# Pooled attention with a SiLU MLP behind it: dummy matmuls tied to a key slot, a fourth PSUM bank for one early group, and two weight loads put ahead of a query load

## The chip, the cores and the metric

The kernel runs on one core of a Trainium2 chip. The metric is the device time of one execution in microseconds (us); smaller is better. The runs of the kernel before took 285.24, 285.42, 285.84 and 285.95 us, median 285.63. One more execution was taken with the hardware profiler, and the views below are of that one.

## The reference

Attention over pooled keys and values, then a two-layer MLP on its output:

```python
k_p = k.reshape(B, H, Sp, pool, D).mean(axis=3)      # B, H = 8, 8; S = 576; D = 64; pool = 8; Sp = 72
v_p = v.reshape(B, H, Sp, pool, D).mean(axis=3)
scores = scale * np.matmul(q, k_p.transpose(0, 1, 3, 2))
...
attn = softmax(scores)
x = np.matmul(attn, v_p)                             # to 4608 x 512
h = x @ w_in                                         # 512 x 2048
g = h * (1.0 / (1.0 + np.exp(-h)))
out = g @ w_out                                      # 2048 x 512
```

The inputs are float32. The kernel works in bfloat16 with float32 accumulation.

## The kernel before, in words

**Tiling.** The 4608 tokens are worked on in nine tiles of 512 (`t` = 0 to 8). For each tile, `up` computes the first product in 16 groups of 128 hidden columns (`plain`, line 541: four matmuls of 128 x 128 weights into one PSUM tile `hp_ps`, then one SiLU activation on ACT, line 547, to `h_T`). Then `down` (tile 0) or `down_quarters` (the others, with seven block products in place of eight) computes the second product. The attention of batch `t + 1` is spread between those matmuls as *fillers*: `spread` runs each filler once the given number of matmul steps has gone by. The order on each engine is the order of the program text; nothing is rescheduled.

**Prologue.** The attention of batch 0 cannot hide behind anything and is computed first, in halves. The raw keys of a batch are 4608 rows (head, pooled row) of 512 values, loaded as five *slots* of 128 rows, the last one with 64. Slots 0 and 1 of the keys come in one transfer on the SP queue, slots 2 and 3 in two transfers on the ACT queue, and slot 4 on SP (lines 700 to 703). `slot_sums` (lines 263 to 272) adds the eight rows of each pooled key on DVE: `slot_sums("k", 0)` takes slots 0 to 2, in place over the first half of each row, then over the first quarter. `select_k` (line 290) places the sums by head on PE, `copy_k` takes them out of PSUM, `q_transpose` (line 153, DVE) turns the queries, `scores` (line 345, PE, then four exponentials on ACT, line 353), `denominators` (line 363, PE; then logarithm and exponential on ACT, or a reciprocal on DVE, line 369), and `numerators` (line 389, PE, then a multiplication on DVE into `xT`, line 398).

**Dummy matmuls.** `warm_up(n)` issues n matmuls of zeros, 128 x 128 weights with 512 columns in bfloat16, into `warm_ps`, which nobody reads. Nineteen stand ahead of `select_k(0, 0)`, and small numbers between the later steps of the prologue.

**PSUM banks.** The eight banks are split in two sets: three for the tag "mm" (`hp_ps`, `warm_ps`, a few of the prologue's tiles) and five for "at" (scores, denominators, numerators, placed keys). Which bank a tile gets is settled when the program is built: the pool gives it the bank that it reckons to be free first. So it isn't a strict rotation. In the program of before, the last four score tiles of the prologue lie in the "at" banks 5, 4, 7 and 3, where a strict order of use would have put 3 before 7. The two denominators that `up` computes for the second halves lie in banks 6 and 5, the numerators behind them in 4 and 7, and in 3 and 6, and the next placed keys in bank 5. The instructions of all engines stand in the program in the order in which the pool's planning took them up; there the second reciprocal (line 369) ends behind the SiLU of the fourth group.

**Tile 0 of `up`.** Its items are groups 0 to 10 on the first 288 tokens, then groups 0 to 10 on the other 224, then groups 11 to 15 on all 512. Its fillers: denominators behind the 2nd and the 6th matmul, numerators behind the 14th and the 18th, placed keys of batch 1 behind the 73rd and the 81st, query transposes behind the 83rd to the 89th. `moe_tables` (line 408) loads the activation table with SiLU just ahead of it.

**The POOL queue.** All other loads are issued by POOL in the order of the text. At the end of the prologue this is: keys of batch 1 in three transfers (lines 767 to 769), `load_q(1)` (576 KB written), `load_w_in(1536, d_ff)` (two transfers of 256 KB; the first-product weights of groups 12 to 15), three quarters of the second-product weights, values of batch 1, the last quarter of the second-product weights.

Of the kernel before, what the change touches and what calls it, by code (L numbers as in the profile page):

```python
# [27 lines left out]
FP32 = mybir.dt.float32  # L28
# [8 lines left out]
def kernel(  # L37
# [9 lines left out]
    nc = tc.nc  # L47
# [6 lines left out]
    d_ff = moe_w_in.shape[1]  # L54
# [27 lines left out]
    singles = ctx.enter_context(tc.tile_pool(name="singles", bufs=1))  # L82
# [8 lines left out]
    def ps_tile(shape, dtype, tag, name):  # L91
        return psum.tile(shape, dtype, tag=tag, bufs=banks[tag], name=name)
# [4 lines left out]
    ident = shifts[:, SP : SP + 128]  # L97
    ones = singles.tile([SP, 32], BF16, name="ones")
    warm = singles.tile([128, 512], BF16, name="warm")
    w_in_sb = singles.tile([128, KF, d_ff], BF16, name="w_in_sb")  # L100
    w_out_sb = singles.tile([128, KG, d_model], BF16, name="w_out_sb")
    w_sum = singles.tile([128, 5, KQ, CQ], BF16, name="w_sum")
# [26 lines left out]
    def load_q(b, halves=False):  # L129
        st = batches.setdefault(b, {})  # L130
        q_bf = mid.tile([128, 2, QI * D], BF16, tag="q_bf", name="q_bf")
        if halves:
            pass
        elif b == B - 1:

            for s in range(4):
                for a in range(2):
                    nc.gpsimd.dma_start(
                        out=q_bf[QP * s : QP * (s + 1), a, :].rearrange(
                            "p (i d) -> p i d", d=D  # L140
                        ),
                        in_=q[b, 4 * a + s].rearrange("(i p) d -> p i d", p=QP),
                    )
        else:
            nc.gpsimd.dma_start(out=q_bf, in_=q_r[b])
        st["q_bf"] = q_bf
        st["qT"] = mid.tile([128, 2, QI, 2, QP], BF16, tag="qT", bufs=1, name="qT")
# [13 lines left out]
    def raw_tile(tag, heads, full=False):  # L161
        raw = big.tile([128, H * PH], FP32, tag=tag, name="raw")
        if full:
            return raw
        return raw[:SP, : H * PH].rearrange("k (h e) -> k h e", h=heads)
# [45 lines left out]
    def k_transpose(b, parts=(0, 1)):  # L211
        st = batches[b]
        kT_ps = ps_tile([128, 2, 2, SP], FP32, "at", "kT_ps")
        for a in parts:
            for c in range(2):
# [10 lines left out]
    RE = POOL * D  # L226
# [7 lines left out]
    SA = SLOTS - 1  # L234
    row_tiles = {
        n: [
            big.tile([128, m, RE], FP32, tag=f"{n}_raw2", name="raw") if i else
            raw_tile(f"{n}_raw", H, full=True)[:, : m * RE].rearrange(
                "r (i e) -> r i e", e=RE
            ) for i, m in enumerate((SA, SLOTS + 1 - SA))  # L240
        ] for n in "kv"
    }


    def load_slots(eng, b, name, i0, i1, half=None):
        es = slice(0, RE) if half is None else slice(half * RE // 2, (half + 1) * RE // 2)
        src = (k if name == "k" else v)[b].rearrange("h (sp p) d -> (h sp) (p d)", p=POOL)
        src = src[:, es]
        how = dict(accum_op=ALU.add) if half else {}
        tiles = row_tiles[name]  # L250
        w = es.stop - es.start
        if i0 == SLOTS:
            eng.dma_start(
                out=tiles[1][:REST, SLOTS - SA, :w], in_=src[128 * SLOTS :], **how
            )
        else:
            j = i0 // SA
            eng.dma_start(
                out=tiles[j][:, i0 - SA * j : i1 - SA * j, :w],
                in_=src[128 * i0 : 128 * i1].rearrange("(i r) e -> r i e", r=128), **how  # L260
            )

    def slot_sums(name, j, halves=False):
        raw = row_tiles[name][j]
        dst = rows5[name][:, SA:] if j else rows5[name][:, :SA]
        w = RE // 4 if halves else RE // 2
        while w > D:
            nc.vector.tensor_add(  # L268
                out=raw[..., :w], in0=raw[..., :w], in1=raw[..., w : 2 * w]
            )  # L270
            w //= 2
        nc.vector.tensor_add(out=dst, in0=raw[..., :D], in1=raw[..., D : 2 * D])
# [131 lines left out]
    def attn_tables():  # L404
        nc.scalar.preload_act_table_set("natural_log_exp_and_others")
# [59 lines left out]
    def up(t, fillers, items):  # L465
# [57 lines left out]
        for it in items:  # L523
            if len(it) == 3:
                plain(t, step, *it)
            else:
                for n in it[1]:
                    stage(it[0], n)
# [1 line left out]
            pass  # L530

    def plain(t, step, g, n0, n):
        hp_ps = ps_tile([128, 512], FP32, "mm", "hp_ps")
        c0 = (t * NTT + n0) % NX

        for r0, r1 in ((0, min(n, NX - c0)), (min(n, NX - c0), n)):
            for kk in range(KF) if r1 > r0 else ():
                if r0 == 0:
                    next(step)
                x0 = (c0 + r0) % NX  # L540
                nc.tensor.matmul(  # L541
                    hp_ps[:, r0:r1],
                    lhsT=w_in_sb[:, kk, g * 128 : (g + 1) * 128],
                    rhs=xT[:, kk, x0 : x0 + r1 - r0],
                    start=(kk == 0), stop=(kk == KF - 1),
                )
        nc.scalar.activation(h_T[:, g, n0 : n0 + n], hp_ps[:, :n], func=AF.Silu)  # L547
# [146 lines left out]
    warm_ps = ps_tile([128, 512], FP32, "mm", "warm_ps")  # L694

    def warm_up(n):
        for _ in range(n):
            nc.tensor.matmul(warm_ps, lhsT=warm[:, :128], rhs=warm, start=True, stop=True)

    load_slots(nc.sync, 0, "k", 0, 2)  # L700
    load_slots(nc.scalar, 0, "k", 2, 3)
    load_slots(nc.scalar, 0, "k", 3, 4)
# [6 lines left out]
    load_slots(nc.gpsimd, 0, "v", 4, 5)  # L709
    attn_tables()  # L710
    nc.vector.memset(warm, 0.0)
    nc.vector.memset(ones, float(POOL))
    nc.vector.memset(kp, 0.0)
    nc.gpsimd.memset(shifts, 0.0)
# [5 lines left out]
    def load_w_in(c0, c1):  # L720
        for g in range(2):
            nc.gpsimd.dma_start(
                out=w_in_sb[:, 2 * g : 2 * g + 2, c0:c1], in_=w_in_r[g][:, :, c0:c1]
            )
# [6 lines left out]
        load_w_in(512 * c, 512 * (c + 1))  # L731

    act_copy = nc.scalar.copy
    warm_up(19)
    slot_sums("k", 0)
    select_k(0, 0)
    copy_k(0, 0, act_copy)
# [29 lines left out]
    load_slots(nc.gpsimd, 1, "k", 0, 3)  # L767
    load_slots(nc.gpsimd, 1, "k", 3, 4)
    load_slots(nc.gpsimd, 1, "k", 4, 5)
    load_q(1)  # L770
    load_w_in(1536, d_ff)
    for c in range(3):
        load_w_out(c)
    load_slots(nc.gpsimd, 1, "v", 0, 3)
# [142 lines left out]
```

The softmax here doesn't subtract the row's maximum and nothing guards it: scores larger than these inputs give would overflow.

## Time and profile before

| what | value |
|---|---|
| median of four runs | 285.63 us |
| the profiled execution's own time | 285.44 us |
| its span, first to last instruction | 283.5 us |
| around the span | 1.94 us |
| PE busy | 276.6 us (98%) |
| DVE busy | 225.6 us (80%) |
| ACT busy | 183.6 us (65%) |
| DMA share, 5 to 40 us | 1.07 to 1.24 of sixteen engines' time |
| mean granted TensorE clock | 1.000 |

Rows of the order-of-time view start with the time from the span's start and the duration, both in us; then engine, line, operation, output and input tiles, shape, how many instructions were merged, and in brackets how long the engine was idle before, and who ended that. The rows of PEld are weight loads, those of PE the matmuls. Durations of matmuls include the way through the array, so the next one starts before the one before has ended: the distance between starts is the rate.

### The profile page before, as it was taken

To read this page: it belongs to the slowest core of one execution; us is meant where nothing else is said; L and a number is where in the kernel's file an instruction comes from. 1 tells how busy PE (TensorE), PEld (TensorE's weight loads), DVE (VectorE), ACT (ScalarE), POOL (GpSimd) and SP (SyncE) were. 2 spreads that over 40 slices of the span, in tenths; PEclk is the share of its full clock that TensorE was granted. 3 is DMA by queue.
4 is the path that set the end of the run, shared out by engine and by line. 5 is a ranking of instruction groups with operands and counts; after the bars stand their busy time and mean duration, and the time that the engine had idled before them with its cause. 6 is when DMAs were issued, how large, how long until landed. Compare 5 with 4: busy or idle time off the path is not lost.

```text
span 283.5 us, 6909 instructions
## 1 busy us (share of the span) xinstructions
PE 276.6 (98%) x2793; PEld 194.4 (69%) x2793; DVE 225.6 (80%) x404; ACT 183.6 (65%) x359; POOL 60.8 (21%) x78
## 2 busy tenths in 40 slices
PE   8889999999999999999999999999999999999995
PEld 2338544466777677767898786688667766787684
DVE  4987836899978898879896988799888786836773
ACT  1667766568567876687668856885779467326700
POOL 8754316242140214021402130541000000000000
PEclk9999999999999999999999999999999999999999
DMA  7999998896739863995498539696830032005003
GB/s 209 281 265 229 214 314 153 233 168 114 148 53 189 187 140 48 177 204 116 66 180 189 104 84 184 128 147 102 148 87 0 2 97 53 2 18 132 1 19 132
DMA packets 31376, 37.70 MB, mean 133 GB/s; under 512 B 10352, under 2 KB 22256, under 8 KB 31344
## 3 DMA queue, kind: packets, MB, share of 16 engines
q0 software_dynamic: 23840, 26.77, 52.5%
q1 hardware_dynamic: 6928, 9.58, 12.5%
q10 hardware_dynamic: 576, 0.92, 0.9%
q8 instruction: 22, 0.36, 0.6%
q14 instruction: 10, 0.08, 0.1%
HBM read 36.70 MB, written 9.44 MB: 163 GB/s over the span
## 4 chain that ended last, share of the span: by engine, by line
PE 90%; DVE 3%; DMA 3%; POOL 1%; ACT 1%; issue 1%; DVEq 0%; POOLq 0%
PE hp_ps L541 25%; PE o_psP L649 15%; PE o_psQ L649 15%; PE u_psP L482 7%; PE u_psQ L482 7%; PE o_psR L649 5%; PE sc_ps L345 4%; PE o_ps L576 3%; DMA raw<-in_v_dram 3%; PE nu_ps L389 2%; PE u_psR L482 2%; PE den_ps L363 2%; DVE xT L398 1%; DVE w_sum L627 1%; POOL q_bf L127 1%
## 5 line engine op out<-in xcount | busy, mean ns | idle before, releaser
L541 PE MATMUL hp_ps<-xT,w_in_sb 128*128 128x512 bf16 (+3 forms) x412 | 82.6, 340 | 0.5 <-ACT h_T L547 0.4
L649 PEld LDWEIGHTS <-h_sum 128*128 128x128 bf16 x640 | 60.6, 98 | 11.9 <-issue 1.3
L547 ACT ACTIVATE h_T<-hp_ps 128x512 bf16<-128x512 f32 (+2 forms) x95 | 51.4, 546 | 25.3 <-PE hp_ps L541 24.2
L541 PEld LDWEIGHTS <-w_in_sb 128*128 128x128 bf16 x412 | 39.4, 98 | 24.9 <-issue 1.4
L609 DVE TENSOR_TENSOR h_sum<-h_T 128x1024 bf16<-128x1024 bf16 (+1 forms) x72 | 50.8, 743 | 6.9 <-ACT h_T L547 6.9
L353 ACT ACTIVATE es<-sc_ps 72x384 bf16<-72x384 f32 (+1 forms) x100 | 39.0, 469 | 10.2 <-PE sc_ps L345 10.1
L482 PEld LDWEIGHTS <-w_sum 128*128 128x128 bf16 x300 | 29.3, 98 | 7.7
L649 PEld LDWEIGHTS <-h_T 128*128 128x128 bf16 x256 | 24.1, 98 | 4.4 <-issue 0.9
L398 DVE TENSOR_TENSOR xT<-nu_ps,rec 128x384 bf16<-128x384 f32 (+1 forms) x50 | 23.9, 531 | 0.2
L372 ACT ACTIVATE lnd<-den_ps 128x384 f32<-128x384 f32 (+1 forms) x23 | 11.1, 484 | 19.3 <-PE den_ps L363 19.3
L153 DVE STREAM_TRANSPOSE qT<-q_bf 128x576 bf16<-128x576 bf16 x32 | 23.0, 754 | 0.1
L490 ACT ACTIVATE h_T<-c_sb 128x512 bf16<-128x512 f32 x30 | 18.1, 626 | 5.7 <-DVE c_sb L514 5.7
L177 POOL DMA_DIRECT2D raw<-in_k_dram x5 | 7.1, 1430 | 52.9 <-DMA raw<-in_k_dram 52.9
L268 DVE TENSOR_TENSOR raw<-raw 128x384 f32<-128x384 f32 (+3 forms) x20 | 12.3, 617 | 7.7 <-DMA raw<-in_v_dram 4.7
L553 POOL DMA_DIRECT2D out_dram<-o_sb x1 | 0.6, 617 | 79.7 <-issue 79.7
L649 PE MATMUL o_psP<-w_out_sb,h_sum 128*128 128x256 bf16 x128 | 17.6, 273 | 0.0
L514 DVE TENSOR_TENSOR c_sb<-u_psP,t_sb 128x512 f32<-128x512 f32 x15 | 10.3, 688 | 8.2 <-PE u_psP L482 3.6
L649 PE MATMUL o_psQ<-w_sum,h_sum 128*128 128x256 bf16 x128 | 16.7, 273 | 0.0
L649 PE MATMUL o_psQ<-w_out_sb,h_sum 128*128 128x256 bf16 x128 | 16.6, 273 | 0.0
L649 PE MATMUL o_psQ<-w_sum,h_T 128*128 128x256 bf16 x128 | 16.5, 273 | 0.0
L649 PE MATMUL o_psP<-w_sum,h_T 128*128 128x256 bf16 x128 | 16.5, 273 | 0.0
L649 PE MATMUL o_psR<-w_sum,h_sum 128*128 128x256 bf16 x128 | 15.7, 273 | 0.0
(80 smaller groups left out, 439.6 us busy)
## 6 DMA issues: line engine op xcount, KB each, us to landing
out_dram<-o_sb SPq DMA_DIRECT2D x128, 64.0 KB, 4.3
raw<-in_k_dram POOLq DMA_DIRECT2D x10, 576.0 KB, 10.0
raw<-in_v_dram POOLq DMA_DIRECT2D x10, 576.0 KB, 8.5
q_bf<-in_q_dram POOLq DMA_DIRECT2D x6, 576.0 KB, 13.6
w_in_sb<-in_moe_w_in_dram POOLq DMA_DIRECT2D x8, 256.0 KB, 8.4
w_out_sb<-in_moe_w_out_dram POOLq DMA_DIRECT2D x4, 512.0 KB, 13.6
raw<-in_v_dram POOLq DMA_DIRECT2D x2, 768.0 KB, 11.3
raw<-in_k_dram POOLq DMA_DIRECT2D x1, 768.0 KB, 10.3
```

Source lines behind the costliest of these rows:

```text
L153: nc.vector.transpose(out=st["qT"][:, a, f * QF : (f + 1) * QF].rearrange("r i c p -> r (i c p)"), in_=st["q_bf"][:, a, f * n : (f + 1) * n],)
L268: nc.vector.tensor_add(out=raw[..., :w], in0=raw[..., :w], in1=raw[..., w : 2 * w])
L345: nc.tensor.matmul(sc[s][:, cs], lhsT=kz[b % 2][rows, g, c, :], rhs=st["qT"][rows, g, i0:i1, c, :], start=(c == 0), stop=(c == 1),)
L353: nc.scalar.activation(es[:, s, :], sc[s], func=AF.Exp, scale=score_scale)
L372: nc.scalar.activation(lnd, den_ps[:, :w], func=AF.Ln)
L398: nc.vector.tensor_mul(out=xT[:, 2 * g0 + c : 2 * (g0 + ng - 1) + c + 1 : 2, cols], in0=nu[c][:, :w].rearrange("r (g n) -> r g n", g=ng), ...
L482: nc.tensor.matmul(ps[bank][:, u, :], lhsT=w[:, kk, 128 * u : 128 * (u + 1)], rhs=x[:, kk, :], start=first and u == 0 and kk == 0, stop=kk ...
L490: nc.scalar.activation(h_T[:, g : g + 2, j * NQ : (j + 1) * NQ], src, func=AF.Silu)
L541: nc.tensor.matmul(hp_ps[:, r0:r1], lhsT=w_in_sb[:, kk, g * 128 : (g + 1) * 128], rhs=xT[:, kk, x0 : x0 + r1 - r0], start=(kk == 0), stop= ...
L547: nc.scalar.activation(h_T[:, g, n0 : n0 + n], hp_ps[:, :n], func=AF.Silu)
L609: nc.vector.tensor_tensor(out=h_sum[n][:, ks, :], in0=quarter(*a, ks), in1=quarter(*b, ks), op=op)
L649: nc.tensor.matmul(ps[b][:, c, :], lhsT=left(n, kt, c), rhs=W_OUT[n][:, kt, :], start=b not in begun, stop=kt == k1 - 1, skip_group_check= ...
```

## The change

Three edits, all around the prologue.

1. Of the 19 dummy matmuls ahead of `select_k(0, 0)`, nine stay. Behind them come eight of a new kind: float32, weights `warm32` (zeros, 128 x 128), with the last 128 columns of slot 2 of the raw keys as the moving operand, still into `warm_ps`. They read what a transfer writes, and so wait for it. `warm32` is set to zero by one more memset on DVE.
2. The `hp_ps` tile of group 3 of tile 0 on its first 288 tokens takes a bank of "at" in place of one of "mm".
3. `load_w_in(1536, d_ff)` is issued ahead of `load_q(1)`.

```diff
+    warm32 = singles.tile([128, 128], FP32, name="warm32")
...
     def plain(t, step, g, n0, n):
-        hp_ps = ps_tile([128, 512], FP32, "mm", "hp_ps")
+        tag = "at" if (t, g, n0) == (0, 3, 0) else "mm"
+        hp_ps = ps_tile([128, 512], FP32, tag, "hp_ps")
...
+    def warm_behind(rhs, n):
+        for _ in range(n):
+            nc.tensor.matmul(
+                warm_ps[:, : rhs.shape[-1]], lhsT=warm32, rhs=rhs, start=True, stop=True
+            )
+
...
     nc.vector.memset(warm, 0.0)
+    nc.vector.memset(warm32, 0.0)
     nc.vector.memset(ones, float(POOL))
...
-    warm_up(19)
+    warm_up(9)
+    warm_behind(row_tiles["k"][0][:, SA - 1, RE - 128 :], 8)
     slot_sums("k", 0)
...
     load_slots(nc.gpsimd, 1, "k", 4, 5)
+    load_w_in(1536, d_ff)
     load_q(1)
-    load_w_in(1536, d_ff)
     for c in range(3):
         load_w_out(c)
```

## The prediction

> **What bounds the kernel now.** I read the chain of work that ended last first, then PE's waits, then the order-of-time view of the two places that the change touches, then the transfers.
>
> ```profile
> PE 90%; DVE 3%; DMA 3%; POOL 1%; ACT 1%; issue 1%; DVEq 0%; POOLq 0%
> ```
>
> ```profile
> PE kz_ps L290 <- DVE k L272: 0.5, 1, 0.5
> PE hp_ps L541 <- ACT h_T L547: 0.4, 1, 0.4
> ```
>
> From about 20 us on the chain is PE nearly without a break, and PE's waits over the whole span list nothing later than the one on `h_T`. So one rule carries the sum: what PE saves or loses by 21.6 us reaches the end at full size, unless something behind it comes late. Before that the chain is not PE's: it runs from the landing of the values at 13.05 over DVE (sums, multiplications, a query transpose) to the last scores at 16.41, four exponentials, the table load, and the first SiLU.
>
> The first place:
>
> ```profile
> 1.20 5.71 PE L698 MATMUL warm_ps<-warm 128*128 128x512 bf16 x19 [1.20 <-DVE warm L711]
> ...
> 4.15 2.26 PEld L698 LDWEIGHTS <-warm 128*128 128x128 bf16 x11 [0.27 <-issue]
> ...
> 5.40 1.55 DVE L268 TENSOR_TENSOR raw<-raw 128x768 f32<-128x768 f32 x2 [2.78 <-DMA raw<-in_k_dram]
> ...
> 6.99 0.36 DVE L272 TENSOR_TENSOR k<-raw 128x192 bf16<-128x192 f32 x1
> ...
> 7.40 0.28 PE L290 MATMUL kz_ps<-shifts,k 128*32 128x72 bf16 x12 [0.50 <-DVE k L272]
> ```
>
> The weight loads of the dummies start 0.43 us apart until 4.15, then eleven start within 2.26 us, 0.215 apart: the array ran at half rate for the first 2.95 us, though the granted-clock row shows 1.00 there, so I go by the spacing. The dummies end at 6.91, and PE waits 0.50 for DVE's key sums. Those began at 5.40, when slots 0 and 1 had landed (issued 0.74, 4.6 us). Nothing that PE does before 7.40 moves 7.40 forward.
>
> The second place:
>
> ```profile
> 17.93 3.77 DVE L369 RECIPROCAL rec<-den_ps 128x288 f32<-128x288 f32 x2 [0.86 <-PE den_ps L363]
> ...
> 18.20 1.28 ACT L408 ACT_TABLE_LOAD   x1
> ...
> 18.64 0.91 PE L541 MATMUL hp_ps<-xT,w_in_sb 128*128 128x288 bf16 x6
> ...
> 19.49 1.01 ACT L547 ACTIVATE h_T<-hp_ps 128x288 bf16<-128x288 f32 x3
> ...
> 19.95 0.41 PE L541 MATMUL hp_ps<-xT,w_in_sb 128*128 128x288 bf16 x2 [0.41 <-ACT h_T L547]
> ...
> 21.11 0.41 ACT L547 ACTIVATE h_T<-hp_ps 128x288 bf16<-128x288 f32 x1 [0.60 <-PE hp_ps L541]
> ...
> 21.24 0.43 PE L389 MATMUL nu_ps<-es,vp 72*32 72x288 bf16 x8
> ...
> 21.61 6.14 PE L541 MATMUL hp_ps<-xT,w_in_sb 128*128 128x288 bf16 x55
> ```
>
> PE has filled three "mm" banks by 19.55 and stands still until the first SiLU, held by the table load, gives one back.
>
> **Part 2, the fourth bank.** Group 3's tile comes from "at" and need not wait. The last six matmuls of the row at 18.64 are 0.12 us apart (288 columns at the 0.215 per 512 of above), so the seventh can start at 18.64 + 6 x 0.12 = 19.36 instead of 19.95. From there the order on PE is unchanged: two matmuls of group 3, numerators, two of group 3, two of group 4, numerators, then the long run that began at 21.60. Shifted by 0.59 this gives 19.36, 19.70, 20.06, 20.65 and 21.01. Two things can hold it. Group 4 takes the bank of group 0, free at 19.91: no wait. The last numerator tile needs an "at" bank, and one tile more is now in that set. The bank that it had, 6, now goes to the tile before it; left are that of the second reciprocal, which ends at 21.70, and group 3's own. Group 3's matmuls end their issue at 20.30; before, a SiLU followed that point by 0.22 (20.89 to 21.11) and took 0.41, so its bank is free at 20.93. In the program of before, the pool's planning puts the SiLU of group 3 ahead of the end of the second reciprocal, so I take group 3's bank. The first half of the numerators ends at 20.65 + 0.18 = 20.83, the second starts at 20.97 and ends at 21.15. The long run starts at 21.15 instead of 21.60: **0.45 us saved**.
>
> What must keep up with a PE that is 0.45 ahead: the multiplications into `xT` end at 23.10, and the items on tokens 288 to 511 begin 26 matmuls into the long run, at 21.15 + 26 x 0.112 = 24.06. Key sums of batch 1 end at 26.45, wanted at 27.67 - 0.45 = 27.22. The last quarter of the second-product weights lands at 28.46 + 14.7 = 43.16 and is wanted by the 37th matmul of the second product, at 42.97 + 5 x 0.213 = 44.04, less 0.45: 43.59. Values of batch 1 are summed at 43.03, wanted (slots 3 and 4) at 45.27 - 0.45 = 44.82. The DVE stretch from 46.29 to 52.6, with work without a gap, starts with a copy that waits for PE, and moves with it. All hold; the tightest by 0.43.
>
> **Part 1, the dummies.** Nine old ones: seven at 0.427 to 4.15 and two at 0.215 end their issue at 4.58. The eight new ones wait for slot 2:
>
> ```profile
> raw<-in_k_dram ACTq DMA_DIRECT2D x1, 256.0 KB, 4.2
> ```
>
> Issued at 0.74, it lands at 4.94; as DVE's sums follow their landing by 0.06, PE goes on at 5.00, after 0.42 us of standing still (shorter than the 0.50 at 7.40, behind which the dummies still start 0.21 to 0.23 apart, so no drop of rate). Behind that wait on PE stands the key placement, wanted at 7.40: 2.40 us for eight matmuls, 0.30 each. No float32 matmul is in the trace. Low end: the shortest stream of 128 x 128 weights, six loads with 64 columns in 0.43 us at 44.21, 0.07 each, taken once: the new ones end at 5.6 and PE waits longer. High end: four passes, each with a load of 0.098 and 128 columns of 0.054 and no overlap, 0.61 each: ends at 9.88. Between them lies four passes at 0.072, 0.29 each, end at 7.32; this I take, since the row is the nearest (the same weights, a short moving operand), and it costs nothing. What covers a later end: delay D goes through placement, scores, exponentials and the value copy on ACT to the first numerators, which end at 13.54 + 0.48 = 14.02 while DVE gets to them at 14.53. So 0.50 is free, and the loss is 8c - 2.40 - 0.50 for a cost c each: none up to c = 0.36, and 1.98 at 0.61.
>
> The Trainium skill speaks against this part. "FP8 and Floating Point Precision", section TensorE Precision Notes, has true float32 take four passes; "TensorE: Matmul & The Clock Gate", section Weight-path perf modes, leaves float32 out of the fast weight load, and its section LDWEIGHTS gives 128/1.2 = 107 ns for a load. No run here shows it yet. An estimate from these: 0.43 each, end at 8.4, a loss of 0.54, which would make the sum 285.53.
>
> The memset of `warm32` takes 0.13 (half of 128x256 in 0.27) on DVE, which then idles 2.78 us before 5.40: nothing; the first dummies wait for the memset ahead of it.
>
> **Part 3, the loads.**
>
> ```profile
> 15.18 0.73 POOL L145 DMA_DIRECT2D q_bf<-in_q_dram  x1 [0.44 <-DMA w_in_sb<-in_moe_w_in_dram]
> 16.51 0.71 POOL L722 DMA_DIRECT2D w_in_sb<-in_moe_w_in_dram  x1 [0.60 <-DMA w_in_sb<-in_moe_w_in_dram]
> 18.76 0.71 POOL L722 DMA_DIRECT2D w_in_sb<-in_moe_w_in_dram  x1 [1.54 <-DMA w_in_sb<-in_moe_w_in_dram]
> ```
>
> These land at 15.18 + 11.7 = 26.9, 16.51 + 11.7 = 28.2 and 18.76 + 10.7 = 29.5. POOL issues one when an earlier one has landed, so the three issue times stay and change owners: weights at 15.18 and 16.51, queries at 18.76, landing about 25.7, 27.0 and 29.5. The weights are first wanted by group 12, at 28.98 + 7 x 0.094 + 4 x 0.216 = 30.5 (30.05 with part 2): before, 1.0 us early, so nothing is gained. The queries are wanted by four DVE transposes at 29.32, now at about 29.55; behind those DVE has weight sums until 35.39 and then 4.31 idle, and PE wants the first two transposes at 34.50, three us later than they end. The same seven transfers follow, in the same places. Zero. Were the cover of the queries gone, it would cost 0.2.
>
> **Sum.** 285.44 - 0.45 + 0 + 0 = 284.99. The profiled execution is 0.19 below the median of the runs; taken off the median it is 285.18. I forecast **285.1**, with its own range 284.7 to 285.5 (0.4 either way: the runs lie within 0.36 of their middle, and part 2's step can be off by some 0.2).
>
> **Rivals.**
>
> *Float32 dummies hold the key placement* (slower). Place: PE between 5.00 and 7.40. From c = 0.42 on it eats the 0.45; at 0.61 the time is 285.44 - 0.45 + 1.98 = 286.97. For it: weights of four bytes and possibly separate passes. Against it: the middle estimate ends at 7.32, 0.58 ahead of the 7.90 from which a delay costs; but 45% more per matmul is enough. 0.22.
>
> *The reciprocal's bank*: the last numerators get the bank of the second denominators and stand until 21.74; the long run starts at 21.92, 0.32 later than before: 285.76. Against it stands the planned order; for it, that one more tile in five banks must displace something. 0.10.
>
> *The edit does nothing*: the tile before the long run still waits for the same table load, and the time is 285.44. Against it: 0.41 idle with nothing else to wait for. 0.06.
>
> *More than the sum*: the rate rose at 4.15 here. In an execution where it rises later, nineteen half-rate dummies would end at 1.20 + 19 x 0.427 = 9.3, 1.9 late, 1.4 beyond the slack; nine end at 5.04, with the slot. The spread of the runs, 0.71, leaves room for it; half of that on top gives 284.6. 0.14.
>
> **Chances.** Forecast 0.48, rivals 0.22, 0.10, 0.06, 0.14. A measurement of this kernel can tell about 0.2%, 0.57 us. The forecast lies just inside that: I give 0.20 of its 0.48 to more than 0.57, all of the last rival and 0.02 for smaller waits elsewhere: faster 0.36. Slower by over 0.57 needs c over 0.49, most of the first rival, 0.19, and 0.03 of the second. Range 284.4 to 286.2: it leaves out c over 0.51.
>
> **What would show it.** Right: no wait of PE on `h_T` near 19.6, the long run at about 21.15, PE's placement of keys still at 7.40. Wrong: a PE wait on the reciprocal near 21; the new dummies ending behind 7.40; a DVE wait for `q_bf` that delays the scores at 34.

## The result, and the profile after

The changed kernel took 285.00 us (median of 31 runs, 284.55 to 285.53), the kernel before on the same chips 285.45 (49 runs, 284.93 to 286.07). The ratio is 0.9982 with a 95% interval of 0.9977 to 0.9987: 0.51 us less, between 0.37 and 0.66. The profiled execution took 284.64, with a span of 282.7.

PE's waits over the whole span of the changed kernel, in us in total, number, and longest:

```profile
PE warm_ps L700 <- DVE warm L719: 1.2, 1, 1.2
PE sc_ps L346 <- DVE qT L154: 0.3, 1, 0.3
PE kz_ps L291 <- DVE k L273: 0.2, 1, 0.2
PE v_ps L309 <- DVE v L273: 0.2, 1, 0.2
PE warm_ps L704 <- DMA raw<-in_k_dram: 0.2, 1, 0.2
PE nu_ps L390 <- DVE vp L316: 0.2, 1, 0.2
```

The wait of `hp_ps` for `h_T` is gone, and none for a reciprocal has come. A new one, for the key slot, is there. The first place, in order of time:

```profile
1.20 3.61 PE L700 MATMUL warm_ps<-warm 128*128 128x512 bf16 x9 [1.20 <-DVE warm L719]
...
5.00 2.02 PE L704 MATMUL warm_ps<-raw,warm 128*128 128x128 f32 x16 [0.20 <-DMA raw<-in_k_dram]
5.28 1.55 DVE L269 TENSOR_TENSOR raw<-raw 128x768 f32<-128x768 f32 x2 [2.51 <-DMA raw<-in_k_dram]
...
7.27 0.28 PE L291 MATMUL kz_ps<-shifts,k 128*32 128x72 bf16 x12 [0.25 <-DVE k L273]
...
12.64 1.15 DVE L269 TENSOR_TENSOR raw<-raw 128x512 f32<-128x512 f32 x2
```

The tied dummies start at 5.00, show as sixteen rows for eight matmuls, and end before the keys are ready; the placement of keys waits for DVE as before. The last row matters for what follows: the sums of the last value slots begin at 12.64 here without a wait for a transfer, and began at 13.14 in the profile before, 0.34 us late for theirs. The second place:

```profile
17.43 3.77 DVE L370 RECIPROCAL rec<-den_ps 128x288 f32<-128x288 f32 x2 [0.86 <-PE den_ps L364]
17.70 1.28 ACT L409 ACT_TABLE_LOAD   x1
18.15 1.15 PE L543 MATMUL hp_ps<-xT,w_in_sb 128*128 128x288 bf16 x8
...
19.00 1.46 ACT L549 ACTIVATE h_T<-hp_ps 128x288 bf16<-128x288 f32 x4
19.23 0.43 PE L390 MATMUL nu_ps<-es,vp 72*32 72x288 bf16 x8
19.59 0.67 PE L543 MATMUL hp_ps<-xT,w_in_sb 128*128 128x288 bf16 x4
...
20.19 0.63 PE L390 MATMUL nu_ps<-es,vp 72*32 72x288 bf16 x8
...
20.75 2.50 PE L543 MATMUL hp_ps<-xT,w_in_sb 128*128 128x288 bf16 x19
```

Six matmuls at 18.64 are now eight at 18.15, with the first two of group 3 and no gap. The last numerators take 0.63 instead of 0.43, since their second half stands for group 3's bank: the last of the four SiLUs at 19.00 ends at 20.46, and the weight loads of that half go on at 20.51:

```profile
20.51 0.10 PEld L390 LDWEIGHTS <-vp 72*32 72x32 bf16 x3 [0.22 <-issue]
```

The long run starts at 20.75 instead of 21.61. But that is 0.86 us, more than the runs gained; 0.49 of it is there already at 18.15, ahead of the bank. So the two profiles can't be set against each other from the span's start. The distance inside this stretch can: from the start of the matmuls ahead of the first SiLU to the long run it is 2.97 before and 2.60 after, and to the placement of keys of batch 1 (at 27.67 and 26.82) it is 9.03 and 8.67.

### The profile page after: what moved, and what is told of

It is laid out like the page before. It is cut to its first block, busy times and chain, and to the rows that moved or that the text cites. A ratio compares the mean times of both kernels' runs of the same rounds, so it can differ in the third digit from the quotient of the medians.

```text
span 282.7 us, 6922 instructions
## 1 busy us (share of the span) xinstructions
PE 276.7 (98%) x2799; PEld 195.3 (69%) x2799; DVE 225.8 (80%) x405; ACT 183.6 (65%) x359; POOL 60.7 (21%) x78
## 4 chain that ended last, share of the span: by engine, by line
PE 80%; DMA 15%; DVE 2%; issue 1%; POOL 1%; POOLq 0%
PE hp_ps L543 21%; PE o_psP L651 15%; PE o_psQ L651 15%; PE u_psP L483 7%; PE u_psQ L483 7%; PE o_psR L651 5%; DMA w_out_sb<-in_moe_w_out_dram 5%; DMA raw<-in_k_dram 4%; DMA q_bf<-in_q_dram 3%; PE sc_ps L346 3%; DMA raw<-in_v_dram 3%; PE u_psR L483 2%; PE nu_ps L390 2%; PE den_ps L364 2%; DVE w_sum L629 1%
## 6 DMA issues: line engine op xcount, KB each, us to landing
raw<-in_k_dram POOLq DMA_DIRECT2D x1, 768.0 KB, 10.2
```

## The experiments

Each kernel was timed beside the kernel before on the same chip. This table has, of each profile: *S*, the start of the matmuls ahead of the first SiLU; the distance from there to the first placement of keys of batch 1; and the rest of the span behind that (from the span with three decimals, as the trace holds it).

| kernel | ratio (95%) | S | S to keys | rest |
|---|---|---|---|---|
| before | 1 | 18.64 | 9.03 | 255.86 |
| changed | 0.9982 (0.9977 to 0.9987) | 18.15 | 8.67 | 255.86 |
| bank alone | 0.9981 (0.9973 to 0.9990) | 18.84 | 8.67 | 255.87 |
| dummies alone | 0.9992 (0.9983 to 1.0001) | 18.24 | 9.04 | 255.67 |
| the same again | 0.9998 (0.9984 to 1.0013) | 18.50 | 9.03 | 255.66 |
| loads alone | 0.9993 (0.9984 to 1.0002) | 18.67 | 9.03 | 255.68 |
| bank and loads | 0.9987 (0.9977 to 0.9997) | 18.76 | 8.67 | 255.85 |
| two banks | 1.0016 (1.0007 to 1.0025) | 18.79 | 9.41 | 255.86 |
| sixteen tied | 1.0039 (1.0026 to 1.0053) | 20.04 | 8.67 | 255.85 |
| nine alone | 1.0064 (1.0038 to 1.0089) | 19.36 | 8.68 | 255.86 |
| late numerators | 0.9975 (0.9965 to 0.9985) | 18.95 | 8.48 | 255.86 |
| four tied | 0.9980 (0.9971 to 0.9989) | 18.14 | 8.67 | 255.85 |
| four tied, late numerators | 0.9976 (0.9966 to 0.9985) | 18.40 | 8.46 | 255.85 |
| nineteen, late numerators | 0.9984 (0.9975 to 0.9993) | 19.19 | 8.47 | 255.87 |

In eleven of the fourteen the rest is 255.85 to 255.87, while the keys are placed anywhere from 26.81 to 28.71. What PE has lost or saved by then does reach the end. In the other three, the dummies alone (twice) and the loads alone, the rest is 0.19 shorter, in two places far behind the change. In the kernel before, denominators and the scores behind them start 0.36 apart near 158 us and 0.38 apart near 217; in these three both distances are 0.27 to 0.28. Kernel before, then the dummies alone:

```profile
158.38 0.43 PE L363 MATMUL den_ps<-es,ones 72*32 72x384 bf16 x4
158.74 0.53 PE L345 MATMUL sc_ps<-qT,kz 32*72 32x192 bf16 x16
```

```profile
157.98 0.35 PE L364 MATMUL den_ps<-es,ones 72*32 72x384 bf16 x4
158.25 0.53 PE L346 MATMUL sc_ps<-qT,kz 32*72 32x192 bf16 x16
```

Neither edit is near these places, and all eleven others have the longer distances. How the two edits come to shift work there isn't shown. But as far as one profile of each tells, 0.19 us of what these three kernels gain (0.07% of the time) is gained there, and not where their edits are meant to act. S moves by 1.9 us, partly by the edit and partly from one execution to the next.

**The bank alone.** The kernel before with this line:

```diff
-        hp_ps = ps_tile([128, 512], FP32, "mm", "hp_ps")
+        tag = "at" if (t, g, n0) == (0, 3, 0) else "mm"
+        hp_ps = ps_tile([128, 512], FP32, tag, "hp_ps")
```

> The kernel before with the fourth bank for group 3 alone. Theory (the bank is the whole gain): the distance from the start of the six to eight matmuls ahead of the first SiLU to the start of the long run of matmuls falls from 2.96 us to 2.60 as in the changed kernel, no PE wait on h_T near 19.6, and the time falls by 0.36 to 0.51 us (ratio 0.9982 to 0.9987). Rival (the dummies or the loads give a part that shows only in the median): the distance falls the same but the time by no more than 0.3 us (ratio 0.9990 or above).

Measured: 2.60 from S to the long run, 8.67 to the keys, ratio 0.9981.

```profile
18.84 1.15 PE L542 MATMUL hp_ps<-xT,w_in_sb 128*128 128x288 bf16 x8
...
21.44 1.77 PE L542 MATMUL hp_ps<-xT,w_in_sb 128*128 128x288 bf16 x13
```

The bank gives what the whole change gives, within the intervals. The profile also caught something that the one before had not. Start of the bank-alone kernel:

```profile
1.20 6.88 PE L699 MATMUL warm_ps<-warm 128*128 128x512 bf16 x19 [1.20 <-DVE warm L712]
...
5.28 1.55 DVE L268 TENSOR_TENSOR raw<-raw 128x768 f32<-128x768 f32 x2 [2.65 <-DMA raw<-in_k_dram]
...
6.62 0.96 PEld L699 LDWEIGHTS <-warm 128*128 128x128 bf16 x5 [0.17 <-issue]
...
8.01 0.28 PE L290 MATMUL kz_ps<-shifts,k 128*32 128x72 bf16 x12
...
12.74 1.15 DVE L268 TENSOR_TENSOR raw<-raw 128x512 f32<-128x512 f32 x2 [0.20 <-DMA raw<-in_v_dram]
...
14.45 0.82 DVE L398 TENSOR_TENSOR xT<-nu_ps,rec 128x288 bf16<-128x288 f32 x2 [0.23 <-PE nu_ps L389]
```

The same nineteen dummies took 6.88 us instead of 5.71: their weight loads stay 0.43 apart until 6.29, not 4.15, and only the last five, from 6.62 on, are 0.22 apart. The keys, summed as early as in the changed kernel, are placed 0.74 later (8.01 against 7.27), and at 14.45 DVE waits for PE's numerators, where before it went from one piece of work to the next.

**The dummies alone, twice.** The kernel before with `warm32`, `warm_up(9)` and the eight tied ones.

> The kernel before with the nine plus eight dummies in place of the nineteen. Theory (nothing but PE's idle time moves): the placement of keys still starts 0.04 us behind DVE's key sums, the new dummies end before 7.0, and the time is the same, ratio 0.9995 to 1.0005. Rival (executions whose rate rises late or whose slots land late gain): ratio 0.9990 to 0.9995, 0.15 to 0.3 us.

> The tied dummies alone once more, the first time at 0.9992 with an interval that reached from 0.9983 to 1.0001. Theory (nothing): 0.9995 to 1.0005. Rival (worth 0.2 us): 0.9988 to 0.9994, and both times together clear of 1.

Measured: 0.9992 and 0.9998. Both intervals hold 1, the second with one run of twelve at 287.24 among others from 284.74 to 285.45. S to the keys is as before. Of each gain 0.19 us, 0.0007 of the ratio, lies in the shorter rest; without it both ratios are within 0.0005 of 1. That favours "nothing", but the intervals still don't exclude 0.2 us.

**The loads alone.** `load_w_in(1536, d_ff)` ahead of `load_q(1)`, nothing else.

> The kernel before with the last first-product weights issued ahead of the queries of batch 1. Theory: DVE waits some 0.2 to 0.8 us for the queries near 29 and nobody waits for DVE; ratio 0.9995 to 1.0005. Rival (the weights were late in some executions, or other transfers land earlier): ratio below 0.9995.

Measured: DVE waits 0.2 us for `q_bf` (0.7 in the changed kernel) and starts the transposes at 29.55 (29.23); PE waits for nothing there. Ratio 0.9993, its interval holds 1, and the shorter rest accounts for it (0.19 us is 0.0007). So nothing here speaks for the rival.

**Bank and loads**, the changed kernel with the nineteen dummies put back:

> The changed kernel with the nineteen dummies of the kernel before: the fourth bank and the moved loads alone. Theory (the dummies' part does nothing): ratio 0.9979 to 0.9987, as the changed kernel. Rival (the tied dummies are worth 0.2 us in the median, because nineteen hold the key placement longer where the rate rises late): ratio 0.9988 to 0.9993.

Measured: 0.9987, on the border of the two expectations; not decided.

**Two banks.** What if the displaced bank isn't free?

```diff
-        tag = "at" if (t, g, n0) == (0, 3, 0) else "mm"
+        tag = "at" if t == 0 and g in (3, 4) and n0 == 0 else "mm"
```

> The changed kernel with group 4 on its first 288 tokens taking an at bank as well. In the built program the last two numerator tiles ahead of the long run then get the bank of group 3 and the bank of the second denominators. Theory (a bank helps only where the bank that it displaces is free in time): the second half of the last numerators stands until the second reciprocal ends, the long run starts 0.6 to 0.8 us later than in the changed kernel against the start of the matmuls ahead of the first SiLU (3.2 to 3.4 us in place of 2.60), and the time is 0.2 to 0.4 us above the kernel before, ratio 1.0007 to 1.0014. Rival (banks are plentiful, two are better than one): ratio 0.9982 or below.

Measured: 1.0016 (1.0007 to 1.0025), a little above the range expected. Three of PE's waits in this kernel:

```profile
PE nu_ps L390 <- DVE rec L370: 0.4, 1, 0.4
PE sc_ps L346 <- DVE qT L154: 0.3, 1, 0.3
PE nu_ps L390 <- ACT h_T L549: 0.3, 1, 0.3
```

and its order of time at the place:

```profile
18.79 1.15 PE L543 MATMUL hp_ps<-xT,w_in_sb 128*128 128x288 bf16 x8
...
21.15 0.31 PE L390 MATMUL nu_ps<-es,vp 72*32 72x288 bf16 x4 [0.25 <-ACT h_T L549]
21.90 0.31 PE L390 MATMUL nu_ps<-es,vp 72*32 72x288 bf16 x4 [0.44 <-DVE rec L370]
22.14 1.03 PE L543 MATMUL hp_ps<-xT,w_in_sb 128*128 128x288 bf16 x7
```

The numerators are torn in two, one half waiting for group 3's SiLU, the other for the reciprocal. The long run starts 3.35 behind S, where 3.2 to 3.4 was expected. This is the prediction's rival of the reciprocal's bank, made real by one bank more.

**Sixteen tied dummies** in place of eight:

> The changed kernel with sixteen float32 dummies in place of eight. In the changed kernel eight took 1.93 us from the landing of slot 2. Theory (a delay of the key placement costs what is beyond 0.5 us of slack at the first numerators): they end about 3.9 us behind the slot, the placement starts 1.5 to 1.7 us later than the key sums allow, and the time is 1.0 to 1.2 us above the changed kernel, ratio to the kernel before about 1.0021. Rival (no slack): 1.6 us above. Rival (the start is the value loads' and not PE's): no more than 0.3 us above.

Measured: 1.0039, against 0.9982 some 1.6 us more than the changed kernel. The order of time:

```profile
1.20 4.02 PE L700 MATMUL warm_ps<-warm 128*128 128x512 bf16 x9 [1.20 <-DVE warm L719]
...
5.01 4.27 PE L704 MATMUL warm_ps<-raw,warm 128*128 128x128 f32 x32
5.19 1.55 DVE L269 TENSOR_TENSOR raw<-raw 128x768 f32<-128x768 f32 x2 [2.42 <-DMA raw<-in_k_dram]
...
9.21 0.28 PE L291 MATMUL kz_ps<-shifts,k 128*32 128x72 bf16 x12
...
13.29 1.15 DVE L269 TENSOR_TENSOR raw<-raw 128x512 f32<-128x512 f32 x2 [0.74 <-DMA raw<-in_v_dram]
...
15.65 0.82 DVE L399 TENSOR_TENSOR xT<-nu_ps,rec 128x288 bf16<-128x288 f32 x2 [0.87 <-PE nu_ps L390]
```

The placement comes 2.03 behind what the key sums allow (5.19 + 1.99 = 7.18, as 5.28 to 7.27 in the changed kernel), and DVE stands 0.87 for the numerators. So the path of the delay is the one predicted. By its size the loss is that of the rival without slack, but the delay was 2.03 and not 1.6, since this execution was at half rate for longer. *S* is 20.04; with the values at 13.29 it would be about 18.79 (in the nine profiles in which the keys were placed on time and no dummy behind them ran at half rate, S follows the start of those sums by 5.50 to 5.53). So 1.25 of the 2.03 were lost in this execution and 0.78 were free. How that goes with a loss of 1.6 in the median is taken up below.

**Nine alone**, with no tied dummies:

> The changed kernel without the eight float32 dummies: PE stands still from 4.6 to about 7.3. Theory (a pause of 2.7 us does not drop the rate, the eight do nothing): the four dummies behind the placement start 0.215 us apart, and the ratio to the kernel before stays at 0.998. Rival (the rate falls in the pause): they start 0.43 us apart, scores and exponentials of the first batch come 1 to 2 us later, and the time is 0.5 to 1.5 us above the changed kernel.

Measured: 1.0064, runs from 286.01 to 288.60. The profiled one is the fastest of the six; what the others lost beyond it no trace shows.

```profile
7.28 0.32 PE L291 MATMUL kz_ps<-shifts,k 128*32 128x72 bf16 x12 [2.06 <-DVE k L273]
7.53 1.89 PE L700 MATMUL warm_ps<-warm 128*128 128x512 bf16 x4
...
14.97 0.82 DVE L399 TENSOR_TENSOR xT<-nu_ps,rec 128x288 bf16<-128x288 f32 x2 [0.52 <-PE nu_ps L390]
```

The placement is in time, but the four dummies behind it take 1.89 instead of 1.04: half rate. All nine had run at half rate in this execution (4.02 us in its profile). So the spacing alone doesn't tell whether the rate fell in the pause or had never risen. The trace also holds records of the granted clock with their times, which the views don't print. In the kernel before the first record of full rate starts at 4.13 us, in the bank-alone kernel at 6.51, each where the spacing changes; here it starts at 10.43, and there is none ahead of it. So the rate had not risen before the pause, and this run doesn't test whether a pause of 2.7 us drops it. What it shows is that some tied dummies are needed once ten of the nineteen are gone.

**Four tied; late numerators; both; nineteen with late numerators.** The second edit moves one filler:

```diff
-            f_up += [(17, lambda: numerators(0, part(1, 1)))]
+            f_up += [(21, lambda: numerators(0, part(1, 1)))]
```

> The changed kernel with the second pair of numerators of the second halves behind the 22nd matmul of tile 0 in place of the 18th, so that group 3's bank is free when they want it. Theory (what is left at this place is the 0.22 us for which the second half of those numerators stands for group 3's SiLU): from the start of the eight matmuls ahead of the first SiLU to the first placement of keys of batch 1 it is 8.45 us in place of 8.67 (9.03 in the kernel before), and the time is 0.2 us below the changed kernel, ratio to the kernel before about 0.9975. Rival (another wait comes in its place, for the multiplications behind the reciprocals): 8.67 or more, ratio 0.998 or above.

> The changed kernel with four float32 dummies in place of eight. In executions whose rate rises early they end near 6.0 and PE stands 1.3 us; where it rises late they end near 7.0 in place of 8.0, and the placement of keys is no longer held. Theory (dummies beyond the key sums cost the part of their delay beyond 0.5 us, some 0.2 us where the rate rises late): ratio to the kernel before 0.9975 to 0.9982. Rival (four are too few to raise or hold the rate, as without any): four dummies behind the placement 0.43 us apart, ratio 1.000 to 1.006.

> Both: four float32 dummies and the late numerators. Theory: the sum of the two, ratio 0.9968 to 0.9975. Rival (too few dummies): as for four alone, less 0.2 us.

> The fourth bank, the loads and the late numerators, but the nineteen bfloat16 dummies of the kernel before. Theory (nine plus eight and nineteen end at the same time in either kind of execution, so this part of the change does nothing): the same as with late numerators and the tied dummies, within 0.15 us. Rival (tied dummies gain): 0.15 to 0.3 us above it.

Measured: late numerators shorten S to the keys by another 0.19 to 0.21, in all three kernels that have them; the ratio of the first is 0.9975, and with four tied dummies 0.9976, just above the 0.9968 to 0.9975 expected of both edits together. Its numerators no longer wait:

```profile
18.95 1.15 PE L543 MATMUL hp_ps<-xT,w_in_sb 128*128 128x288 bf16 x8
20.04 0.43 PE L390 MATMUL nu_ps<-es,vp 72*32 72x288 bf16 x8
20.40 1.15 PE L543 MATMUL hp_ps<-xT,w_in_sb 128*128 128x288 bf16 x8
21.48 0.43 PE L390 MATMUL nu_ps<-es,vp 72*32 72x288 bf16 x8
21.85 1.40 PE L543 MATMUL hp_ps<-xT,w_in_sb 128*128 128x288 bf16 x10
```

Both numerators take 0.43 again. Four tied dummies do as well as eight (0.9980), so the fear that four are too few found no support. With four, an execution in which all nine ran at half rate still placed the keys on time:

```profile
1.20 4.02 PE L700 MATMUL warm_ps<-warm 128*128 128x512 bf16 x9 [1.20 <-DVE warm L719]
...
5.01 1.77 PE L704 MATMUL warm_ps<-raw,warm 128*128 128x128 f32 x8
...
7.30 0.28 PE L291 MATMUL kz_ps<-shifts,k 128*32 128x72 bf16 x12 [0.52 <-DVE k L273]
```

Nineteen with late numerators came out at 0.9984, not clear of 0.9975; in the median it is 0.14 us above the kernel with eight tied dummies, on the border of the two expectations. Its execution was the latest of all:

```profile
1.20 7.23 PE L700 MATMUL warm_ps<-warm 128*128 128x512 bf16 x19 [1.20 <-DVE warm L719]
...
8.36 0.28 PE L291 MATMUL kz_ps<-shifts,k 128*32 128x72 bf16 x12
```

The keys, wanted at 5.31 + 1.99 = 7.30, are placed 1.06 late. The two kernels with late numerators and tied dummies have the lowest medians of those timed beside them (284.66 us each, against 285.39 for the kernel before and 284.83 with four tied dummies). Against the changed kernel the intervals overlap; what is shown is the 0.2 us in the distance.

## Why the prediction was right, point by point

**Right: what reaches the end.** The rule that PE's gains and losses by 21.6 us arrive at full size holds: the rest of the span is the same within 0.02 us in eleven profiles. The three others differ by 0.19 us in places that the change doesn't touch.

**Right in mechanism, a fifth too large: the bank.** The prediction put the long run at 21.15, 2.51 behind 18.64; it is 2.60, so 0.36 are saved and not 0.45. The mis-sized term is the numerators behind the bank wait: their second half was to start 2.33 behind S and end 0.18 later; its weight loads start at 20.51, 2.36 behind S, and the next matmul starts 0.24 after those. A half that starts by itself took 0.24 where half of an unbroken set of eight takes 0.18. The choice of bank was the important step: that the last numerators get group 3's bank, so that the reciprocal (to 21.20) doesn't hold them, is what the changed program has; with two banks they do get the reciprocal's, and the sign turns.

**Partly luck: the time.** The sum had a gain of 0.45 and the runs gained 0.51 (0.37 to 0.66), but the trace accounts for 0.36 only, just below that interval. Where the remaining 0.15 comes from is not shown; the bank alone, with the nineteen old dummies, gained as much in the runs (0.54, between 0.29 and 0.77). The forecast of 285.1 for the time also started from four runs of the kernel before with a median of 285.63; all 49 have 285.45. It came within 0.1 of the measured 285.00 because it was set between the 284.99 of the profile and the 285.18 of that median.

**Right for the profile, too narrow for the runs: the dummies.** Their sixteen rows start 0.11 apart (the first two 0.19; the last starts at 6.75), so eight took 1.9 us, 0.22 each behind the first, against the 0.29 taken. In the changed kernel's profile the first rival (0.42 or more each) is out. It is not out where the array is at half rate: in the two-banks kernel the first eleven rows start 0.21 to 0.22 apart (the first two 0.27), 0.43 for a matmul, and the keys were placed 0.73 us late. Against nineteen old dummies even that is no loss: in the last profile shown, where the half rate ended as late, they placed the keys 1.06 late. Two statements were too simple. The half-rate time was taken from one profile as 2.95 us. Among the profiles with nineteen dummies it ended near 4.2 in three, at 6.5 in the bank-alone kernel and at 7.2 in the last one shown, and five of the nine others ran all of the first nine at half rate. And the 0.50 us of slack belongs to an execution in which the values are there at 13.14. In the bank-alone kernel the sums of the last values began at 12.74, as in the dummies-alone kernel, whose S is 18.24; S is 18.84, so of a delay of 0.74 only 0.14 was free. By the same reckoning 0.18 of 0.73 was free with two banks (12.74) and 0.15 of 1.06 with nineteen and late numerators (12.78). The slack goes with the lateness of the values: 0.14 to 0.18 near 12.75, the predicted 0.50 at 13.14, 0.78 at 13.29. That fits a larger loss with sixteen dummies in executions with earlier values, though which values the timed executions had isn't known.

**The rival "more than the sum"** had the right premise, shown in those profiles, and too high a price, as the tied dummies run at half rate too: in the two-banks kernel they took 3.02 us, and the keys were placed at 7.96, about as late as with nineteen in the bank-alone kernel (8.01). What part 1 is worth in the median stays open. Four comparisons differ by it alone, in the mean against the kernel before: the dummies alone, -0.30 and -0.12 us; the change and the bank with the loads, -0.52 and -0.39; late numerators with tied dummies and with nineteen, -0.60 and -0.49. From the first pair 0.19 must be taken for the shorter rest, which leaves -0.11 and +0.07 (-0.11 without the run at 287.24); the other two differ by 0.13 and 0.11. So they lean to a gain of about 0.1, and none is clear of zero; the change against the bank alone (-0.52 and -0.57), where the loads differ too, leans the other way.

**Right: the loads.** The weights land at 14.86 + 10.2 = 25.1 and 16.33 + 10.0 = 26.3, the queries at 18.33 + 10.9 = 29.2, near the 25.7, 27.0 and 29.5 of the prediction. DVE waits for them and nobody waits for DVE.

**The rule that spoke against it.** The Trainium skill, "FP8 and Floating Point Precision", section TensorE Precision Notes, has true float32 take four passes. The trace shows two rows of weight loads and two of matmuls for each, 0.11 apart at full rate, 0.22 for a matmul. That agrees with four passes of 128 columns: four times the 0.054 that 128 columns take in the old dummies (0.215 for 512) is 0.215. At half rate it is 0.43 against 0.427. So one tied dummy costs as much as one old one, at either rate. What failed is the estimate, 0.43, that put a whole weight load of "TensorE: Matmul & The Clock Gate", section LDWEIGHTS, on each of the four passes: at full rate the measured time leaves no room for them. The measurement decides: at full rate the cost was half of the estimate, which is why the part cost nothing in this profile.

**The two profiles.** Of the 0.86 us between their long runs 0.37 is the bank; 0.49 is that S came earlier, with the values of that execution (their sums began 0.50 earlier). It would have been a mistake to give it to the dummies: S lies at 18.24 and at 18.50 in two executions of one kernel.

## What to carry to other kernels

When a tile takes a bank from another set, ask which tile gets which bank next and when its last reader ends: one bank more gave 0.36 us, two gave a loss, and moving one consumer behind the free point gave another 0.2. To tell an edit of a fraction of a microsecond from the scatter of executions, measure distances between two events inside one trace, on both sides of the edit, and check that what lies behind stays equal: here three kernels were 0.19 us shorter in places that their edits don't touch. A slack read from one execution is the slack of that execution: name the event that makes it, here a transfer, and ask when else that can land.

## What the runs showed of the hardware

- The moment at which the array goes from half to full rate varied from 4.13 to 7.22 us in the prologues with nineteen dummies, with busy matmuls from 1.20 on. With nine matmuls and a pause of 2.06 us it was 10.43, and four matmuls at 7.5 us still ran 0.43 us apart. The granted-clock row showed 1.00 throughout, as the trace has no clock record for the time ahead of that moment; the spacing shows it, and so does the start of the first record.
- A float32 matmul with 128 x 128 weights and 128 columns shows as two loads and two matmuls and takes 0.22 us at full rate and 0.43 at half, as long as a bfloat16 one with 512 columns (0.215 and 0.427); eight of them show from 5.00 to 7.02, and in an execution with half rate for most of them from 5.01 to 8.03.
- The sums of the last values, which follow a transfer from the same queue in the same order, began anywhere from 12.61 to 13.45 us.
